# Second-network gate from SBUF sums, and five row blocks in place of six after the first two

## The chip, the cores and the metric

One Trainium2 chip, one core of it. The kernel is written in Python for Bass with the Tile layer, which allocates buffers and sets the semaphores. The metric is device time in microseconds (us), the median of a few runs. The engines are named as in the profile: PE is TensorE's matmul, PEld its weight load, DVE is VectorE, ACT is ScalarE, POOL is GpSimd, and SP is SyncE, which issues most DMAs.

## The reference, cut to what matters

Three networks follow one another on 2304 tokens (4 batches of 576) of 512 values.

```python
attn = softmax(mask(q @ k.T / 8))              # 8 heads of 64; 32 keys each, every key or every 4th
x = attn @ v                                   # as 2304 x 512
xn = x / sqrt(mean(x * x) + 1e-6) * rms_g      # first network
x = (silu(xn @ w_gate) * (xn @ w_val)) @ w_out     # 512 -> 1536 -> 512
logits = x @ w_gate2                           # the gate: 512 -> 8 experts
P = exp(logits - logits.max())                 # second network
for _ in range(8):
    P /= P.sum(1, keepdims=True) + 1e-9
    P /= P.sum(0, keepdims=True) + 1e-9
    P *= 2304 / 8
out = sum(P[:, e:e+1] * (relu(x @ w1[e]) @ w2[e]) for e in range(8))   # 512 -> 1024 -> 512
```

All is fp32. Matmul operands are split into a high and a low part in the rounded type fp32r, and a product is three matmuls: high by high, high by low, low by high.

## The kernel before, in words

**First phase.** Attention makes rows in tiles of 128 tokens (five tiles a batch, the fifth with 64), and writes them, normalised, transposed and split, into `xn`, the input of the first network. The first network works on blocks of tokens: two to a batch, 256 and 320 wide, eight in all. `gemm_h(blk, f)` makes one slice of 128 of the 1536 hidden values: 12 matmuls for `pg`, 12 for `pv` (L456), then Silu on ACT (L468), a product on DVE (L469), the high part on ACT (L470) and the low part on POOL (L471). `gemm_out(blk, c)` (L430) multiplies four such slices by `w_out`: 12 matmuls for each quarter `dc` of the 512 outputs, whose sums are collected in the tile `partial` by ACT (L439) or DVE (L441). After the third of three such chunks the sums are written to `x2d` in HBM (L443). Each matmul's moving operand is as wide as its block, and a block costs 12 x 24 + 3 x 4 x 12 = 432 matmuls.

**Order.** The first two blocks take turns chunk by chunk while their weights are still being converted (`split_double`: each half weight is loaded into a word buffer, and passes ACT, DVE and POOL by way of one of three buffers `m`; the conversion of the last ten weights loads from L345 into four word buffers). From block 2 on, a block's matmuls are the main line, and side lines are spread along them: the attention of the next block (`block_att`), a gate, and 24 steps of `weight_sums` a block. `weight_sums` has 64 items (load half a megabyte, three operations on POOL L645 to L653, one on DVE, store at L655) and takes 129 steps; it uses three large buffers, `kbd`, `vbd` and `conv`. Apart from SP's queue in the first part, which is in program order, a planner sets each engine's order when the kernel is built, by program order and its own estimates of when operands are ready; it brings ready work forward. On the chip each engine then runs its instructions in that order. `xn` of block i+2 has the buffer of block i.

**The gate.** `gate(blk)` takes 384 tokens. For each quarter it loads the sums back from `x2d` (L577, tile `sx`), makes the high part on ACT (L585) and the low part on POOL (L586), and multiplies both by the gate's weights (L592, tile `pl`, 16 outputs: a high and a low half). The 16 rows are copied (L599), transposed (L604) and written to `L2` (L605). Five gates run in the first phase; the sixth, `last_gate`, stands at the head of the second phase (loads L886, high parts on ACT L887, low parts on DVE L888, matmuls L898), since the last block's sums must first be in HBM.

**Second phase.** `gemm1` and `gemm2` (L1007, L1060) go through 48 units, 384 and 256 columns wide, with the gate's P computed on the side and needed from the fifth unit on. Weights are loaded and split unit by unit (L662, L676, L677), and stored split (L707). Its pools lie where those of the first phase lay, the tiles `h_a`, `h_s` over `kbd`, `vbd`, `conv` and `xn`, and wait for each of them.

Of the kernel before, what the change touches and what calls it, by code (L numbers as in the profile page):

```python
# [10 lines left out]
ALU = mybir.AluOpType  # L11
# [18 lines left out]
def attention_moe_kernel(  # L30
# [33 lines left out]
    wgs = cpool.tile([P, 4, NE], F32, name="wgs")  # L64
    wg = cpool.tile([P, 4, 2, NE], F32R, name="wg")
    L2 = cpool.tile([P, NTT, 16], F32, name="L2")
# [88 lines left out]
    def att_tile(n, xn, c0, bufs, after_qk=None, after_pv=None):  # L155
# [142 lines left out]
        for h in range(2):  # L298
            src = psT[:, halves[h]].rearrange("p (k n) -> p k n", k=2)
            hi, lo = (xn[:, 2 * h : 2 * h + 2, s, c0 : c0 + nn] for s in range(2))  # L300
# [21 lines left out]
    def split_double(pool, src, name, gk, number, hi_eng, lo_eng):  # L322
# [96 lines left out]

    def gemm_out(blk, c):  # L420
        tok0, n, _ = blocks[blk]
        if c == 0:
            partials[blk] = mpool.tile([P, 4, n], F32, tag=f"partial{blk % 2}", name=f"partial_{blk}", bufs=1)
        partial = partials[blk]
        for dc in range(4):
# [16 lines left out]
            if c == 2:  # L442
                nc.sync.dma_start(x2d[dc, :, tok0 : tok0 + n], partial[:, dc, :])  # L443
            yield

    def gemm_h(blk, f):
# [19 lines left out]
        h = mpool.tile([P, 2, 320], F32R, tag="h", name=f"h_{blk}_{f}", bufs=5)  # L466
        hf = mpool.tile([P, 320], F32, tag="hf", name=f"hf_{blk}_{f}", bufs=2)[:, :n]
# [104 lines left out]
    def gate(blk):  # L572

        pl = ps_o.tile([P, 512], F32, tag="o", name=f"pl_{blk}")
        def load(kt):
            st = stg.tile([P, 512], F32, tag="st", name=f"sx_{blk}_{kt}", bufs=3)[:, :TH]
            nc.sync.dma_start(st, x2d[kt, :, TH * blk : TH * blk + TH])  # L577
            return st

        st = load(0)  # L580
        yield
        k = 0
        for kt in range(4):
            hi, lo = (stg.tile([P, 512], F32R, tag="st", name=f"g{s}_{blk}_{kt}", bufs=3)[:, :TH] for s in range(2))
            nc.scalar.copy(hi, st)  # L585
            nc.gpsimd.tensor_tensor(out=lo, in0=st, in1=hi.bitcast(F32), op=ALU.subtract)  # L586
            for _ in range(3):
                yield
            if kt < 3:
                st = load(kt + 1)  # L590
            for x in (hi, lo):
                nc.tensor.matmul(  # L592
                    pl[:16, :TH], lhsT=wg[:, kt].rearrange("p s e -> p (s e)"), rhs=x, start=k == 0, stop=k == 7
                )
                k += 1
            for _ in range(3):
                yield
        lg = stg.tile([16, 512], F32, tag="st", name=f"lg_{blk}", bufs=3)
        nc.scalar.copy(lg[:, :TH], pl[:16, :TH])  # L599
        yield  # L600
        ptl = ps_o.tile([P, 512], F32, tag="o", name=f"ptl_{blk}")
        nt = TH // P
        for j in range(nt):
            nc.tensor.transpose(ptl[:, j * 16 : j * 16 + 16], lg[:, j * P : j * P + P], id16)  # L604
        nc.vector.tensor_copy(  # L605
            L2[:, nt * blk : nt * blk + nt, :], ptl[:, : nt * 16].rearrange("p (t e) -> p t e", e=16)
        )
# [126 lines left out]
    for b in range(B):  # L734
        blocks.append((b * S, 256, [(5 * b, 0), (5 * b + 1, 128)]))
# [499 lines left out]
```

## Time and profile before

| | us |
|---|---|
| median of 3 runs (2062.46 to 2068.68) | 2067.11 |
| the profiled execution's own time | 2064.67 |
| its span, first to last instruction | 2062.8 |
| PE busy in the span | 2005.0 (97%) |
| DVE, POOL, ACT busy | 1392.5, 1217.0, 1093.6 |

The times are those of whole executions; the span is what the profiler saw of one. The first phase ends, and the second begins, at 612 us of the span. A row of a view gives a group of instructions with their count, their busy time and the idle time ahead of them, or one stretch of time with each engine's busy part in it; PE's granted clock is given as a share of 2.4 GHz.

### The profile page before, as it was taken

How to read it: one execution, taken by the hardware profiler on the slowest of the kernel's cores; microseconds unless marked ns; L12 is line 12 of the kernel's file. 1: busy time of each engine (PE TensorE's matmuls, PEld its weight loads, DVE VectorE, ACT ScalarE, POOL GpSimd, SP SyncE). 2: the span in 40 equal slices, each digit the busy share in tenths (PEclk: the TensorE clock that was granted, in tenths of full speed). 3: DMA queues.
4: the chain of work that ended last, by engine and by line, in shares of the span. 5: the costliest groups of instructions: out<-in, count | busy, mean ns of one | idle time of the engine just before them, and what ended most of it. 6: DMA issues, size and time to landing. Idle time of an engine off the chain costs nothing.

```text
span 2062.8 us, 42661 instructions
## 1 busy us (share of the span) xinstructions
PE 2005.0 (97%) x16102; PEld 1967.9 (95%) x16102; DVE 1392.5 (68%) x2884; ACT 1093.6 (53%) x2408; POOL 1217.0 (59%) x1182
## 2 busy tenths in 40 slices
PE   6899999999999999999999999999999999999999
PEld 4788999999998999999999999999999999999999
DVE  7985443534347898787877676766776576667666
ACT  5664443433347566666665555555555654555453
POOL 4785555655646677778776454455545544554452
PEclk9999999999999999999999999999999999999999
DMA  9423777676556667877889667667677666566652
GB/s 270 168 83 125 252 238 245 227 239 248 212 181 250 234 242 290 305 278 275 296 321 359 198 197 233 205 203 226 220 247 268 220 205 203 181 198 205 204 175 82
DMA packets 210014, 464.68 MB, mean 225 GB/s; under 512 B 17168, under 2 KB 59920, under 8 KB 209808
## 3 DMA queue, kind: packets, MB, share of 16 engines
q1 hardware_dynamic: 202752, 442.97, 63.1%
q10 hardware_dynamic: 7056, 18.98, 2.8%
q8 instruction: 127, 2.08, 0.4%
q14 instruction: 79, 0.65, 0.1%
HBM read 349.16 MB, written 112.72 MB: 224 GB/s over the span
## 4 chain that ended last, share of the span: by engine, by line
PE 75%; DVE 8%; DMA 6%; ACT 4%; POOL 3%; issue 2%; SPq 1%; ACTq 0%; DVEq 0%; POOLq 0%
PE ya L1060 18%; PE pa L1007 17%; PE yb L1060 9%; PE pb L1007 8%; PE po L430 5%; PE pg L456 5%; PE pv L456 5%; PE pc L1007 4%; PE yc L1060 4%; DMA sx<-x2d 1%; DVE h_a L978 1%; DMA w0r<-in_w 1%; DMA x2d<-partial 1%; DMA kbd<-in_kt 1%; SPq L145 0%
## 5 line engine op out<-in xcount | busy, mean ns | idle before, releaser
L677 POOL TENSOR_TENSOR w_s<-w0s,w_s 128x512 fp32r<-128x512 f32 x192 | 261.0, 1360 | 91.3 <-ACT w_s L676 89.7
L986 POOL TENSOR_TENSOR h_s<-p,h_s 128x384 fp32r<-128x384 f32 x96 | 105.2, 1117 | 324.5 <-ACT h_s L985 271.1
L1096 DVE SCALAR_TENSOR_TENSOR acc<-ya,Pm,acc 128x256 f32<-128x256 f32 x510 | 221.8, 477 | 65.1 <-PE ya L1060 64.9
L677 POOL TENSOR_TENSOR w_a<-w0r,w_a 128x512 fp32r<-128x512 f32 x144 | 193.8, 1349 | 114.8 <-ACT w_a L676 108.1
L1007 PE MATMUL pa<-x_t,w_s 128*128 128x384 f32 x1152 | 224.3, 335 | 1.9 <-ACT p L1019 1.9
L1060 PE MATMUL ya<-w_t,h_s 128*128 128x256 f32 x1728 | 225.2, 282 | 0.6 <-ACT acc L1085 0.5
L1060 PEld LDWEIGHTS ya<-w_t,h_s 128*128 128x128 f32 x1728 | 218.8, 190 | 1.4 <-ACT acc L1085 0.8
L1007 PEld LDWEIGHTS pa<-x_t,w_s 128*128 128x128 f32 x1152 | 197.3, 188 | 2.3 <-ACT p L1019 2.1
L456 PE MATMUL pv<-xn,w_v 128*128 128x320 f32 (+1 forms) x1152 | 184.4, 302 | 10.7 <-DVE w_v L375 2.6
L456 PE MATMUL pg<-xn,w_g 128*128 128x320 f32 (+1 forms) x1152 | 183.7, 301 | 2.6 <-ACT hf L468 1.4
L430 PE MATMUL po<-h,w_o 128*128 128x320 f32 (+1 forms) x1152 | 175.0, 298 | 4.8 <-DVE partial L441 1.6
L456 PEld LDWEIGHTS pv<-xn,w_v 128*128 128x128 f32 x1152 | 164.2, 191 | 15.6 <-ACT hf L468 3.8
L676 ACT CAST w_s<-w0s 128x512 fp32r<-128x512 f32 x192 | 119.9, 625 | 108.2 <-PE pb L1007 66.4
L1096 DVE SCALAR_TENSOR_TENSOR acc<-yb,Pm,acc 128x256 f32<-128x256 f32 x258 | 109.7, 476 | 93.4 <-PE yb L1060 93.3
L456 PEld LDWEIGHTS pg<-xn,w_g 128*128 128x128 f32 x1152 | 163.3, 191 | 6.2 <-ACT hf L468 1.7
L430 PEld LDWEIGHTS po<-h,w_o 128*128 128x128 f32 x1152 | 159.4, 188 | 8.2 <-DVE partial L441 2.0
L471 POOL TENSOR_TENSOR h<-hf,h 128x256 fp32r<-128x256 f32 (+1 forms) x96 | 80.5, 840 | 100.2 <-ACT h L470 99.6
L986 POOL TENSOR_TENSOR h_s<-r,h_s 128x384 fp32r<-128x384 f32 x96 | 96.8, 1031 | 61.2 <-ACT h_s L985 57.3
L1060 PE MATMUL yc<-w_b,h_a 128*128 128x256 f32 x864 | 122.7, 283 | 0.0
L1060 PE MATMUL yb<-w_t,h_s 128*128 128x256 f32 x864 | 120.9, 281 | 0.0
L1060 PE MATMUL yb<-w_t,h_a 128*128 128x256 f32 x864 | 120.6, 282 | 0.3 <-DVE acc L1089 0.3
L1007 PE MATMUL pc<-x_b,w_a 128*128 128x384 f32 x576 | 116.4, 337 | 2.8 <-DVE h_s L986 2.7
(253 smaller groups left out, 4718.1 us busy)
## 6 DMA issues: line engine op xcount, KB each, us to landing
w_t<-split SPq DMA_DIRECT2D x128, 512.0 KB, 4.3
w0r<-in_w SPq DMA_DIRECT2D x96, 512.0 KB, 6.1
w0s<-sums SPq DMA_DIRECT2D x96, 512.0 KB, 7.5
w_b<-split SPq DMA_DIRECT2D x96, 512.0 KB, 3.8
split<-w_t SPq DMA_DIRECT2D x64, 512.0 KB, 2.9
split<-w_b SPq DMA_DIRECT2D x48, 512.0 KB, 3.6
w1r<-in_w SPq DMA_DIRECT2D x32, 512.0 KB, 5.4
w1s<-sums SPq DMA_DIRECT2D x32, 512.0 KB, 7.2
```

The costliest lines, as they stand in the source:

```text
L430: nc.tensor.matmul(po[:, :n], lhsT=ow[f][:, a, dc * P : dc * P + P], rhs=hs[blk, f][:, bb, :n], start=k == 0, stop=k == 11,)
L456: nc.tensor.matmul(ps[:, :n], lhsT=w[kt, fg][:, a, fo * P : fo * P + P], rhs=xn[:, kt, bb, :n], start=k == 0, stop=k == 11,)
L471: late_g = nc.gpsimd.tensor_tensor(out=h[:, 1, :n], in0=hf, in1=h[:, 0, :n].bitcast(F32), op=ALU.subtract)
L676: nc.scalar.copy(v[:, :, 0, :], src)
L677: lo_eng.tensor_tensor(out=v[:, :, 1, :], in0=src, in1=v[:, :, 0, :].bitcast(F32), op=ALU.subtract)
L978: nc.vector.scalar_tensor_tensor(out=h[:, 1, :], in0=src, scalar=0.0, in1=h[:, 0, :].bitcast(F32), op0=ALU.max, op1=ALU.subtract)
L986: eng.tensor_tensor(out=h[:, 1, :], in0=src, in1=h[:, 0, :].bitcast(F32), op=ALU.subtract)
L1007: nc.tensor.matmul(ps, lhsT=w1s[u, a][:, kt, hl, q * P : q * P + P], rhs=xc[b, kt][:, xl, :TH], start=fresh and k == 0, stop=k == 5, skip_ ...
L1060: nc.tensor.matmul(ps, lhsT=hh[u, a, q][:, hl, jj * P : jj * P + P], rhs=w2s[u, b][:, q, wl, :], start=fresh and k == 0 and jj != 1, stop= ...
L1096: nc.vector.scalar_tensor_tensor(out=dst, in0=ps, scalar=scale, in1=dst, op0=ALU.mult, op1=ALU.add)
```

## The change

The blocks from the second batch on are made of other tiles: 384, 320, 384, 320 and 320 tokens instead of six of 256 and 320, so seven blocks instead of eight (the first two stay). The gate works on a block, not on 384 tokens, from the block's sums while these are in SBUF: as each quarter is done, ACT and POOL split it into the block's own `xn`, whose rows are no longer needed (block 0's go through staging buffers instead). The sums of all blocks but the first share one buffer `partial`; the first block's lie in a part of `vbd`. `L2` holds the logits after the sum of their two halves, so the second phase needs no sum of its own. The sixth gate becomes the seventh block's own, in the first phase. `weight_sums` keeps its 24 steps a block. The word buffers of the last weights become three, in `kbd` and `conv`. Block 2's attention, now three tiles, runs beside the last chunks of blocks 0 and 1 rather than between them. In P's iterations four steps instead of three stand ahead of each matmul.

```diff
@@ split_double: word buffers of the last ten weights
-                if (2 * number + j) % 4 < 3:
-                    words = stg.tile([P, 512], U32, tag="st", name=f"sd_{name}_{j}", bufs=3)
-                else:
-                    words = conv[:, :512].bitcast(U32)
+                slot = (2 * number + j) % 3
+                words = (conv[:, :512] if slot == 2 else set0.spare[0][:, 512 * slot : 512 * slot + 512]).bitcast(U32)
@@ gemm_out
+    def split_partial(blk, dc, hi, lo):
+        src = partials[blk][:, dc, :]
+        nc.scalar.copy(hi, src)
+        nc.gpsimd.tensor_tensor(out=lo, in0=src, in1=hi.bitcast(F32), op=ALU.subtract)
+    def gate_step():
+        if gates and next(gates[0], run) is run:
+            gates.pop(0)
...
-            partials[blk] = mpool.tile([P, 4, n], F32, tag=f"partial{blk % 2}", name=f"partial_{blk}", bufs=1)
+            if blk == 0:
+                partials[blk] = set0.spare[1].rearrange("p (d n) -> p d n", d=4)
+            else:
+                partials[blk] = mpool.tile([P, 4, BIG[0]], F32, tag="partial", name=f"partial_{blk}", bufs=1)[:, :, :n]
...
             if c == 2:
                 nc.sync.dma_start(x2d[dc, :, tok0 : tok0 + n], partial[:, dc, :])
-            yield
+                if blk > 0:
+                    split_partial(blk, dc, xns[blk][:, dc, 0, :n], xns[blk][:, dc, 1, :n])
+            yield
+        if c == 2:
+            gates.append(gate(blk))
@@ gemm_h: hf moves to the staging buffers
-        hf = mpool.tile([P, 320], F32, tag="hf", name=f"hf_{blk}_{f}", bufs=2)[:, :n]
+        hf = stg.tile([P, 512], F32, tag="st", name=f"hf_{blk}_{f}", bufs=3)[:, :n]
@@ moe1_chunks
                 yield from gemm_h(blk, f)
+                if blk > 1:
+                    gate_step()
                 if pending:
                     yield from gemm_out(*pending.pop())
             pending.append((blk, c))
-        if chunks[-1] == (7, 2):
+        if chunks[-1] == (NB - 1, 2):
             yield from gemm_out(*pending.pop())
+            while gates:
+                gate_step()
@@ gate(blk): load, split and product of 384 tokens become a product from xn
-            st = stg.tile([P, 512], F32, tag="st", name=f"sx_{blk}_{kt}", bufs=3)[:, :TH]
-            nc.sync.dma_start(st, x2d[kt, :, TH * blk : TH * blk + TH])
-            nc.scalar.copy(hi, st)
-            nc.gpsimd.tensor_tensor(out=lo, in0=st, in1=hi.bitcast(F32), op=ALU.subtract)
+                rhs = parts[kt][:, n * hl : n * hl + n] if blk == 0 else xns[blk][:, kt, hl, :n]
+                nc.tensor.matmul(
+                    pl[:16, :n], lhsT=wg[:, kt].rearrange("p s e -> p (s e)"), rhs=rhs,
+                    start=kt == hl == 0, stop=kt == 3 and hl == 1,
+                )
...
+            nc.vector.reduce_sum(
+                out=L2[a:b, t0 + j : t0 + k, :], in_=pair.rearrange("p t s e -> p t e s"), axis=AX.X
+            )
@@ blocks
-        blocks.append((b * S, 256, [(5 * b, 0), (5 * b + 1, 128)]))
-        blocks.append((b * S + 256, 320, [(5 * b + 2, 0), (5 * b + 3, 128), (5 * b + 4, 256)]))
+    for tiles in ((0, 1), (2, 3, 4), (5, 6, 7), (8, 9, 10), (11, 12, 13), (14, 15, 16), (17, 18, 19)):
...
+    BIG = (384, 320)
@@ order
-    run(moe1_chunks([(0, 2)]))
     next_psum()
-    run(block_att(2))
-    run(moe1_chunks([(1, 2)]))
+    third = block_att(2)
+    for step_, _ in enumerate(moe1_chunks([(0, 2), (1, 2)])):
+        if step_ % 2 == 0 and step_ < 10 or step_ > 10:
+            next(third, None)
+    run(third)
...
-    for i in range(2, 8):
+    for _ in range(3):
+        gate_step()
+    for i in range(2, NB):
         sides = [(some(sgen1, 24), 24)]
...
@@ side(): the last gate goes
-    def last_gate():
...
-        yield from last_gate()
-        nc.vector.tensor_tensor(out=Pm, in0=L2[:, :, 0:8], in1=L2[:, :, 8:16], op=ALU.add)
+        for _ in range(4):
+            yield
```

## Rows read from the trace of the kernel before

**Rows 1.** Page, part 5, costliest groups: one of three such groups (pg, pv, po)

```profile
L456 PE MATMUL pg<-xn,w_g 128*128 128x320 f32 (+1 forms) x1152 | 183.7, 301 | 2.6 <-ACT hf L468 1.4
```

**Rows 2.** Chain that ended last, in time: start us, us, what (widths 256, 320, 384)

```profile
372.86 1.44 PE pv L456 x12
...
589.76 1.76 PE pg L456 x12
...
699.39 2.08 PE pa L1007 x12
```

**Rows 3.** Stretches at the phases' boundary: engines' busy us, PE's clock, DMA share, GB/s

```profile
612.00:622.80 10.80, 10.80 (x63) 10.52 (x61) 2.08 (x4) 4.60 (x10) 3.61 (x4) 1.00 1.04 402
622.80:629.60 6.80, 2.03 (x6) 0.35 (x5) 5.13 (x5) 5.56 (x12) 6.80 (x6) 0.75 0.82 300
629.60:633.10 3.50, 3.47 (x11) 3.47 (x12) 3.42 (x7) 3.49 (x9) 3.50 (x3) 0.50 0.87 287
```

**Rows 4.** Chain that ended last, 600 to 645 us

```profile
610.66 8.43 DMA x2d<-partial
...
619.15 5.65 DMA sx<-x2d
...
626.41 3.17 DVE xg L888 x2
```

**Rows 5.** Timeline of PE, 622 to 640 us: start, us, what, idle before and releaser

```profile
625.39 0.35 PE L898 MATMUL pl_last<-xg,wg 128*16 128x384 f32 x1 [2.55 <-ACT xg L887]
...
629.93 3.71 PE L1007 MATMUL pa<-x_b,w_s 128*128 128x384 f32 x12
```

**Rows 6.** Groups by line and form: the gate's matmuls, in the phase and at its end

```profile
L592 PE MATMUL pl<-g,wg 128*16 128x384 f32 x40 | 10.7, 337 | 0.0
...
L898 PE MATMUL pl_last<-xg,wg 128*16 128x384 f32 x8 | 3.2, 447 | 4.8 <-ACT xg L887 2.6 <-DVE xg L888 2.2
```

**Rows 7.** Waits, 180 to 640 us: total us, times, longest

```profile
ACT g L585 <- DMA sx<-x2d: 22.0, 8, 5.9
```

**Rows 8.** Waits of PE alone, 180 to 612 us

```profile
PE psR L286 <- ACT psX L278: 2.6, 1, 2.6
PE psXT L297 <- DVE xs L291: 1.9, 2, 1.1
```

**Rows 9.** Tile sx: low parts on POOL and on DVE, ns min/median/max

```profile
L586 POOL TENSOR_TENSOR g<-sx,g x20: 1007/1018/1470, 204.2 to 579.3; 128x384 fp32r<-128x384 f32 x20
...
L888 DVE TENSOR_TENSOR xg<-sx,xg x4: 549/1364/1627, 625.4 to 630.6; 128x384 fp32r<-128x384 f32 x4
```

**Rows 10.** Timeline of SP, 137 to 172 us: loads into one word buffer of four

```profile
143.72 0.33 SPq L345 DMA_DIRECT2D conv<-in_w_val  x1
...
151.68 0.33 SPq L345 DMA_DIRECT2D conv<-in_w_val  x1
```

**Rows 11.** Timeline of ACT, 140 to 153 us: first use of one buffer m, twice

```profile
142.91 0.44 ACT L355 ACTIVATE conv<-sd_v 128x256 f32<-128x256 f32 x1 [0.45 <-DVE w_g L375]
...
151.07 0.44 ACT L355 ACTIVATE conv<-sd_v 128x256 f32<-128x256 f32 x1 [0.94 <-DVE w_v L375]
```

**Rows 12.** Timeline of PE, 165 to 210 us: tile 6's transposes, block 2's first matmul

```profile
190.11 0.60 PE L297 MATMUL psXT<-cst,xs 128*128 128x128 f32 x4
...
192.17 0.38 PE L456 MATMUL pg<-xn,w_g 128*128 128x256 f32 x1
```

**Rows 13.** Timeline of DVE, 186 to 222 us: last writes of tiles 6 and 7

```profile
192.40 0.62 DVE L307 TENSOR_TENSOR xn<-psXT,xn 128x256 fp32r<-128x256 f32 x1
...
219.96 0.63 DVE L307 TENSOR_TENSOR xn<-psXT,xn 128x256 fp32r<-128x256 f32 x1 [1.17 <-ACT xn L306]
```

**Rows 14.** A stretch ahead of block 2, columns as in Rows 3

```profile
180.00:190.00 10.00, 9.44 (x71) 9.24 (x71) 2.80 (x8) 2.21 (x8) 3.83 (x6) 1.00 0.49 155
```

**Rows 15.** Lines L653 and L655, weight sums: the last item's operation; stores' landing

```profile
L653 POOL TENSOR_TENSOR kbd<-kbd x11: 732/738/1190, 224.5 to 565.0; 128x256 f32<-128x256 f32 x11
...
DMA to landing us min/median/max: 2.6/3.9/7.6
```

More of the change, by code (lines that the diff above doesn't have):

```diff
@@ L299, in att_tile @@
             src = psT[:, halves[h]].rearrange("p (k n) -> p k n", k=2)
-            hi, lo = (xn[:, 2 * h : 2 * h + 2, s, c0 : c0 + nn] for s in range(2))
+            dst = xn() if callable(xn) else xn
+            hi, lo = (dst[:, 2 * h : 2 * h + 2, s, c0 : c0 + nn] for s in range(2))
             if h == 0:
@@ L598, in gate @@
[L598 to L607, printed above, removed]
+        tok0, n, _ = blocks[blk]
@@ new lines, in gate, with product @@
+        if blk == 0:
+            parts = [stg.tile([P, 512], F32R, tag="st", name=f"gp_{blk}_{kt}", bufs=3) for kt in range(3)]
+            parts.append(parts[0])
+        pool, kw = (ps_o, dict(tag="o")) if blk < NB - 1 else (ps_a, dict(tag="single", bufs=1))
+        pl = pool.tile([P, 512], F32, name=f"pl_{blk}", **kw)
+        def product(kt):
+            for hl in range(2):
+                rhs = parts[kt][:, n * hl : n * hl + n] if blk == 0 else xns[blk][:, kt, hl, :n]
[3 more added lines that the diff above has]
+                )
@@ new lines, in gate @@
+        if blk == 0:
+            for kt in range(3):
+                split_partial(blk, kt, parts[kt][:, :n], parts[kt][:, n : 2 * n])
+            yield
+            product(0)
+            parts[3] = stg.tile([P, 512], F32R, tag="st", name=f"gp_{blk}_3", bufs=3)
+            split_partial(blk, 3, parts[3][:, :n], parts[3][:, n : 2 * n])
+            yield
+        for kt in range(1 if blk == 0 else 0, 4):
+            product(kt)
+        yield
+        off = tok0 % P
+        lg = stg.tile([16, 512], F32, tag="st", name=f"lg_{blk}", bufs=3)
@@ new lines, in gate @@
+        if off:
+            nc.gpsimd.memset(lg[:, :off], 0.0)
+        nc.scalar.copy(lg[:, off : off + n], pl[:16, :n])
+        yield
+        ptl = pool.tile([P, 512], F32, name=f"ptl_{blk}", **kw)
+        t0, nt = tok0 // P, -(-(off + n) // P)
+        spans = []
+        for j in range(nt):
+            w = min(P, off + n - P * j)
+            nc.tensor.transpose(ptl[:w, j * 16 : j * 16 + 16], lg[:, j * P : j * P + w], id16)
+            spans.append((off if j == 0 else 0, w))
+        j = 0
@@ L733, in attention_moe_kernel @@
     blocks = []
-    for b in range(B):
-        blocks.append((b * S, 256, [(5 * b, 0), (5 * b + 1, 128)]))
-        blocks.append((b * S + 256, 320, [(5 * b + 2, 0), (5 * b + 3, 128), (5 * b + 4, 256)]))
+    for tiles in ((0, 1), (2, 3, 4), (5, 6, 7), (8, 9, 10), (11, 12, 13), (14, 15, 16), (17, 18, 19)):
+        n, tl = 0, []
+        for tn in tiles:
+            tl.append((tn, n))
+            n += P if tn % 5 < 4 else P // 2
+        blocks.append((sum(bl[1] for bl in blocks), n, tl))
+    NB = len(blocks)
+    BIG = (384, 320)
     xns = {}
@@ L740, in block_att, with xn @@
         tok0, n, tl = blocks[i]
-        xns[i] = mpool.tile([P, 4, 2, n], F32R, tag=f"xn{i % 2}", name=f"xn_{i}", bufs=1)
+        def xn():
+            if i not in xns:
+                xns[i] = mpool.tile([P, 4, 2, BIG[i % 2]], F32R, tag=f"xn{i % 2}", name=f"xn_{i}", bufs=1)
+            return xns[i]
         for tn, c0 in tl:
@@ L947, in side @@
             nc.vector.reduce_sum(out=csum, in_=Pm.rearrange("p t e -> p e t"), axis=AX.X)
-            for _ in range(3):
+            for _ in range(4):
                 yield
```

82 lines of the change are left out of this document (18 added, 64 removed).

## The prediction

> **What bounds the kernel now.** I read the page first: PE is busy 97% of the span, and part 2 shows it at 9 tenths or more in every slice after the first two. So time is won in two ways alone, by less PE work or by closing the few gaps in PE's stream. The work that the change touches is three groups of 1152 matmuls, 3456 in all [rows 1], that is 8 blocks of 432. The chain gives what a closed group of twelve costs: 1.44 us at 256 columns, 1.76 at 320, 2.08 at 384 [rows 2], so 120.0, 146.7 and 173.3 ns a matmul. Each 64 columns add 26.7 ns, and what is left at no columns is 120.0 - 4 x 26.7 = 13.3 ns: a fixed cost of every matmul.
>
> The windows show the largest gap. From 622.8 to 629.6 us, just after the second phase begins, PE is busy 2.03 of 6.80 us at a granted clock of 0.75, and from 629.6 to 633.1 the clock is 0.50, its level of 1.2 GHz, after PE had been idle [rows 3]. The chain names the cause: the last sums' way to HBM (8.43 us), back (5.65), and their split [rows 4]. PE stood 4.8 us ahead of the last gate's matmuls [rows 6], and the twelve matmuls behind them took 3.71 us [rows 5] against 2.08 [rows 2]: 4.8 + 1.6 = 6.4 us lost.
>
> Elsewhere in the first phase the waits view shows ACT held 22.0 us by the gate's loads [rows 7], but PE itself waited little from 180 to 612 us: 2.6 us for a square on ACT and 1.9 for the normalised rows are its longest [rows 8]. So that ACT wait is mostly off the path.
>
> **The change, part by part.**
>
> *Fewer matmuls.* Seven blocks for eight make 432 fewer, over the same columns: 432 x 13.3 = 5.76 us less PE work. In the stretch of blocks 2 and later PE has no cover for it to vanish in, so I take it whole: **-5.8**. The Trainium skill, TensorE: Matmul & The Clock Gate, section "Back-to-back issue gap", gives the gap between warm matmuls as N / 2.4 + 2.5 ns. By it the saving would be an estimated 432 x 2.5 = 1.1 us, and the whole sum below -3.6 instead of -8.3. The fixed part measured here, over three widths, is 13.3 ns; so the trace doesn't agree with the 2.5.
>
> *The last gate from SBUF.* Four stores to HBM stay, but nobody waits for them at the boundary; four loads of 0.2 MB go, and ACT no longer stands in its queue ahead of the evictions of `pa`. In their place the last block's quarters are split as they come, a copy of about 0.5 us on ACT and a subtraction of about 1.0 us on POOL [rows 9], while PE has the second phase's first unit, 84 matmuls of 173 ns, 14.6 us, to go on with. The matmuls themselves weigh the same: 48 of 384 columns cost 8.3 us, 56 of the new widths 8 x (120 + 4 x 146.7 + 2 x 173.3) ns = 8.4; three more transposes and the added waits in P's loop I put at 0.3. **+0.4**. The 6.4 us of the gap could all come back.
>
> *The weight sums run over.* They take 129 steps; six blocks of 24 gave 144, five give 120. Before, the last item ended at 566 us [rows 15], 46 us ahead of the boundary. Now five of 64 items are left, and their POOL and DVE work is tied behind the last `gemm_h`. That is 15 operations of 0.74 us on POOL [rows 15], 11.1 us, three loads and five stores of 0.52 MB, 4.2 MB against the 0.8 MB of the gate's loads that go. They land where the DMA engines are already at 1.04 and move 402 GB/s [rows 3]: 3.4 MB more is 8.5 us of their time. Behind them in the queues stand the second unit's weight loads on SP and splits on POOL, which PE needs some 15 us after the boundary. Also `h_a`, `h_s` lie over `kbd`, `vbd` and `conv` and wait for the last stores, of up to 7.6 us each [rows 15]; other slots, over `xn` and the attention's buffers, are free at once, so the first of them need not wait. Lower bound nothing (all within the 14.6 us), upper the full 8.5 us and the half clock again, 1.6. I take 2.5, as the first unit covers most of it. Boundary together: -6.4 + 2.5 = **-3.9**. The Trainium skill, GPSIMD Engine Reference, section "Key points", says that GpSimd shares its SBUF interfaces with VectorE and contends with its two-input instructions. The trace agrees: a two-input subtraction on DVE ranged from 549 to 1627 ns [rows 9] where POOL was busy throughout [rows 3]. Four such operations stretched to the longest would add an estimated 4.3 us, with a sum of -4.0; that is weight for the rival that the boundary refills.
>
> *ACT and POOL in the blocks.* 28 copies and subtractions of block width replace 24 of each sort at 384; their inputs come from a DVE addition instead of a DMA of several us. PE's waits of 1.9 us [rows 8] may go in part: between 0 and -1.9, **-1.0**. The single `partial` buffer must be read out before the next block's first sums; four slices of `gemm_h`, 96 matmuls of 147 ns or 14 us, lie between, against stores that land in 8.43 us at the slowest [rows 4]: nothing. If a store were later than that, PE's evictions would wait for it on ACT.
>
> *Three word buffers for four.* Now one of the four comes round in 8.0 us [rows 10], 2.0 us a half weight. If the same round held three, each half would take 2.65, and the nine halves up to the last `w_val` would come 6 us later: the upper bound. But the buffers `m` are three already, and one of them is reused after 8.2 us, with ACT waiting for DVE to leave it [rows 11]: that ring is the tighter one, 2.7 us a half. So near the lower end of 0: **+0.5**.
>
> *Three attention tiles before block 2.* Block 2 needed two, and started 2.1 us after the last of them was transposed [rows 12], with PE never idle. Tile 7 now stands ahead too; in the trace it ended 27.6 us behind tile 6 [rows 13]. Cover after 192.2 us: block 1's last sums, 48 x 146.7 = 7.0 us, tile 7's own matmuls, an estimated 3.0 us (five groups like the 0.60 us of its transposes), and block 0's gate, 8 x 0.12 = 1.0: until 203.2 us. At the pace of before tile 7 would end at 220.6, idle 17.4 us; at best it is hidden. In the ten us ahead of block 2 DVE, ACT and POOL were busy 2.80, 2.21 and 3.83 of 10 [rows 14]: the tile's pace there was set by its place in the order, not by an engine. In the new order its instructions precede the end of block 1, and PE has nothing better. I estimate 12.3 us for it, less than half, so **+1.5**.
>
> **Sum:** -5.8 + 0.4 - 3.9 - 1.0 + 0.5 + 1.5 = -8.3 us, on the profiled execution 2064.7 - 8.3 = 2056.4. That execution is 2.4 us below the median of the three runs, so as a median 2058.8.
>
> **The rivals.**
>
> *A. The boundary refills (same).* The five late items and the loads behind them cost PE about what the last gate did. For: DMA share 1.04 there; against: 14.6 us of independent matmuls. Time: 2058.8 + 3.9 = 2062.7.
>
> *B. All gaps close (faster).* The 6.4 us come back whole, the psXT wait of 1.9 goes, tile 7 and the words are hidden, and so is the single PE wait of 2.6 us [rows 8] with a half clock behind it of 1.6: that one came from `weight_sums`, whose first items now run elsewhere. -5.8 + 0.4 - 6.4 - 1.9 - 4.2 = -17.9: 2049.2. Against: planned orders make new gaps where they close old ones.
>
> *C. The attention is the bound before block 2 (slower).* Tile 7 keeps its 27.6 us: PE idles 17.4 us and pays 1.6 at the half clock, 17.5 more than the 1.5 taken: 2076.3. It decides from about 8 us of idle, tile 7's end at 212, where the gain is gone; from 218 the change is slower by over 0.3%.
>
> *D. The fixed part stays (same).* If what is constant in a matmul were not paid by the count, wider blocks would bring nothing: 2058.8 + 5.8 = 2064.6. Against: three widths lie on one line [rows 2]. This is where the section on the issue gap, cited above, would lead.
>
> **How the numbers follow.** 0.3% is 6.2 us, about what a measurement of this kernel can tell from no change. Forecast 0.42, own range 2053 to 2061; A 0.22; B 0.16; C 0.15; D 0.05. Faster: the forecast and B, 0.58. Same: A and D, 0.27. Slower: C, 0.15. The range holds the forecast, A, D, most of B and none of C's far end: 2048 to 2070.
>
> **What would show it.** In the changed profile: 3024 matmuls in the three groups, twelve still at 1.44, 1.76 and 2.08 us; no idle PE ahead of `pl` at the boundary, and a clock of 1.00 there; weight sums (L653's successor) after the last `gemm_h`, and PE waits, if any, for splits on POOL or `w0r`, `w1s` landings (A); the stretch from block 1's last slice to block 2's first matmul without idle PE (C would show PE waiting for `xn` or `xs`); loads into word buffers still 2 to 2.7 us apart. The prediction would be wrong if PE stood for more than 5 us ahead of block 2, or if the second phase's first units waited longer than the last gate had made them.

## The result and the profile after

The change made the kernel slower: a median of 2085.77 us over 4 runs (2081.62 to 2089.48) against 2067.89 us for the kernel before (4 runs). The ratio is 1.0101, with a 95% interval of 1.0083 to 1.0119. The forecast was 2058.8 us, with a range of 2048 to 2070.

The page of the changed kernel, head and part 1, then two groups of part 5, which answer to [rows 1], and the group `po` of the kernel before:

```profile
span 2087.7 us, 41709 instructions
...
PE 2011.7 (96%) x15681; PEld 1973.5 (95%) x15681; DVE 1388.8 (67%) x2866; ACT 1088.1 (52%) x2383; POOL 1214.6 (58%) x1181
...
L442 PE MATMUL po<-h,w_o 128*128 128x320 f32 (+2 forms) x1008 | 177.3, 324 | 11.8 <-POOL h L487 5.2
L472 PE MATMUL pg<-xn,w_g 128*128 128x320 f32 (+2 forms) x1008 | 180.3, 321 | 4.9 <-DVE hf L485 2.1
```

```profile
L430 PE MATMUL po<-h,w_o 128*128 128x320 f32 (+1 forms) x1152 | 175.0, 298 | 4.8 <-DVE partial L441 1.6
```

Three groups of 1008 are the 3024 matmuls forecast. The number behind the last bar is PE's idle time ahead of the group: `po` waited 4.8 us before and waits 11.8 us now, 5.2 of them for POOL. The chain that ended last shows what twelve matmuls cost (start us, us, what), beside a group of the second phase:

```profile
223.44 2.12 PE pv L472 x12
...
305.94 1.76 PE pv L472 x12
...
695.38 2.08 PE pa L1014 x12
```

Against [rows 2], 320 columns cost the same; 384 columns cost 2.12 us in the first phase and 2.08 in the second.

The boundary of the phases is where the time went. The timeline of PE from 595 to 660 us (start, us, what, idle before and releaser in brackets):

```profile
604.67 1.97 PE L442 MATMUL po<-h,w_o 128*128 128x320 f32 x6 [2.78 <-POOL h L487]
...
611.37 3.57 PE L442 MATMUL po<-h,w_o 128*128 128x320 f32 x12 [2.45 <-DVE partial L453]
...
634.63 0.59 PE L932 MATMUL pr<-idp,gm 128*1 128x128 f32 x2 [3.99 <-DMA idp<-in_consts]
...
657.78 2.50 PE L1067 MATMUL ya<-w_b,h_a 128*128 128x256 f32 x10 [14.66 <-ACT h_a L984]
```

The timeline of ACT, 655 to 660 us, says what `h_a` waited for:

```profile
657.24 0.87 ACT L984 ACTIVATE h_a<-pc 128x384 fp32r<-128x384 f32 x2 [16.17 <-DMA sums<-conv]
```

The chain from 612 to 662 us shows how that came about:

```profile
612.99 7.68 DMA sums<-vbd
620.69 8.04 DMA vbd<-in_w
...
628.79 0.75 POOL vbd L681
...
646.36 0.68 POOL conv L689
647.04 0.32 POOL kbd L689
647.36 9.78 DMA sums<-conv
657.24 0.50 ACT h_a L984
657.78 4.21 PE ya L1067 x18
```

A store has to leave `vbd` before the next item is loaded there. The late items' operations stand between splits of weights on POOL, and the last store from `conv`, that of the last item but one, lands at 657.1 us. Only then may ACT write the first `h_a`, which lies over that buffer. The tile view of `sums`, 590 to 665 us, answers to [rows 15]: a store's landing had a median of 3.9 us over the first phase of the kernel before and has 7.2 here.

```profile
L691 SPq DMA_DIRECT2D sums<-conv x2: 319/365/411, 618.1 to 647.4; - x2
...
DMA to landing us min/median/max: 3.3/7.2/10.5
```

Windows of the changed kernel (us, then busy us of PE, PEld, DVE, ACT, POOL with counts, PE's granted clock, DMA share, GB/s):

```profile
220.00:575.00 355.00, 355.00 (x3595) 343.02 (x3595) 143.99 (x292) 130.37 (x265) 193.79 (x249) 1.00 0.60 206
575.00:600.00 25.00, 22.42 (x149) 21.48 (x147) 22.27 (x32) 11.85 (x27) 19.33 (x18) 1.00 0.79 269
600.00:620.00 20.00, 13.46 (x56) 12.02 (x57) 7.19 (x8) 6.03 (x12) 18.48 (x22) 0.66 0.84 274
620.00:640.00 20.00, 14.85 (x74) 13.59 (x73) 7.85 (x18) 10.14 (x20) 10.96 (x13) 0.87 0.90 345
640.00:660.00 20.00, 5.34 (x24) 5.02 (x24) 4.55 (x9) 3.23 (x9) 7.72 (x8) 0.67 0.68 236
```

The gap of before at 623 to 633 us [rows 3] is closed: `pl` of the last block has no idle PE ahead of it. Three others took its place, each with a stretch at the lower level of the clock behind it. The middle of the first phase got better: PE is never idle from 220 to 575 us, against 348.06 busy of 355 before, and both waits of [rows 8] are gone.

To add this up I use one measure: **lost time** is the length of a stretch less what the matmuls that start in it cost at the full clock, 13.3 ns and 26.7 ns for each 64 columns [rows 2] (short ones at a flat 60 ns, the attention's, several of which run side by side, at 12 ns; these are the same in all kernels). By this measure all matmuls cost 1952.2 us before and 1946.8 after, 5.4 us less. Lost, in us, in the profiled executions:

| kernel | 0–220 | 220–575 | 575–700 | 700–2000 |
|---|---|---|---|---|
| before | 58.8 | 26.8 | 12.2 | 8.1 |
| after | 65.0 | 17.7 | 41.4 | 12.3 |
| after − before | +6.2 | −9.1 | **+29.2** | +4.2 |

The differences make +30.5 us, less 5.4 of matmuls +25.1; the spans differ by 24.9 (2087.7 − 2062.8). The medians differ by 17.9: the profile after is 3.7 us above its median, that of before 3.2 below its own. How finely a column can be read: eight kernels with one and the same program up to about 200 us, of those below, lost 61.3 to 65.5 us in the first. A row is no count of idle time: after the change PE is never idle from 220 to 575 us, and the 17.7 us stand for what these prices leave out, so that only differences between kernels say something.

### The profile page after: what moved, and what is told of

It is laid out like the page before. It is cut to its first block, busy times and chain, and to the rows that moved or that the text cites. A ratio compares the mean times of both kernels' runs of the same rounds, so it can differ in the third digit from the quotient of the medians.

```text
span 2087.7 us, 41709 instructions
## 1 busy us (share of the span) xinstructions
PE 2011.7 (96%) x15681; PEld 1973.5 (95%) x15681; DVE 1388.8 (67%) x2866; ACT 1088.1 (52%) x2383; POOL 1214.6 (58%) x1181
## 4 chain that ended last, share of the span: by engine, by line
PE 79%; DVE 6%; DMA 6%; POOL 3%; issue 2%; ACT 2%; SPq 1%; ACTq 0%; DVEq 0%; POOLq 0%
PE ya L1067 17%; PE pa L1014 16%; PE yb L1067 9%; PE pb L1014 8%; PE pg L472 6%; PE pv L472 6%; PE po L442 6%; PE pc L1014 4%; PE yc L1067 4%; DMA w0r<-in_w 2%; POOL w_s L713 1%; POOL w_t L713 1%; DMA xr<-x2d 1%; PE psS L175 1%; PE psX L239 1%
## 5 line engine op out<-in xcount | busy, mean ns | idle before, releaser
L442 PE MATMUL po<-h,w_o 128*128 128x320 f32 (+2 forms) x1008 | 177.3, 324 | 11.8 <-POOL h L487 5.2
L472 PE MATMUL pg<-xn,w_g 128*128 128x320 f32 (+2 forms) x1008 | 180.3, 321 | 4.9 <-DVE hf L485 2.1
L472 PE MATMUL pv<-xn,w_v 128*128 128x320 f32 (+2 forms) x1008 | 180.2, 321 | 4.3 <-DVE w_v L373 2.5
L472 PEld LDWEIGHTS pv<-xn,w_v 128*128 128x128 f32 x1008 | 158.8, 191 | 8.9 <-DVE w_v L373 3.6
L472 PEld LDWEIGHTS pg<-xn,w_g 128*128 128x128 f32 x1008 | 158.5, 192 | 8.6 <-DVE hf L485 2.8
L487 POOL TENSOR_TENSOR h<-hf,h 128x320 fp32r<-128x320 f32 (+2 forms) x84 | 77.6, 925 | 131.6 <-ACT h L486 131.5
L993 POOL TENSOR_TENSOR h_s<-r,h_s 128x384 fp32r<-128x384 f32 x96 | 96.3, 1025 | 63.6 <-ACT h_s L992 59.3
L1067 PE MATMUL ya<-w_b,h_a 128*128 128x256 f32 x864 | 115.7, 285 | 14.7 <-ACT h_a L984 14.7
L1067 PEld LDWEIGHTS ya<-w_b,h_a 128*128 128x128 f32 x864 | 112.5, 193 | 15.0 <-ACT h_a L984 15.0
```

The lines of the kernel that those rows point to most:

```text
L442: nc.tensor.matmul(po[:, :n], lhsT=ow[f][:, a, dc * P : dc * P + P], rhs=hs[blk, f][:, bb, :n], start=k == 0, stop=k == 11,)
L472: nc.tensor.matmul(ps[:, :n], lhsT=w[kt, fg][:, a, fo * P : fo * P + P], rhs=xn[:, kt, bb, :n], start=k == 0, stop=k == 11,)
L487: late_g = nc.gpsimd.tensor_tensor(out=h[:, 1, :n], in0=hf, in1=h[:, 0, :n].bitcast(F32), op=ALU.subtract)
L993: eng.tensor_tensor(out=h[:, 1, :], in0=src, in1=h[:, 0, :].bitcast(F32), op=ALU.subtract)
L1067: nc.tensor.matmul(ps, lhsT=hh[u, a, q][:, hl, jj * P : jj * P + P], rhs=w2s[u, b][:, q, wl, :], start=fresh and k == 0 and jj != 1, stop= ...
```

## The experiments

Lost time by stretch, in us, beside the ratio to the kernel before with its interval:

| kernel | 0–220 | 220–575 | 575–700 | 700–2000 | ratio |
|---|---|---|---|---|---|
| after, 30 steps a block | 64.4 | 31.2 | 10.3 | 16.2 | 1.0036 (1.0023–1.0049) |
| before, 20 steps a block | 57.5 | 21.3 | 35.8 | 10.0 | 1.0073 (1.0058–1.0088) |
| after, late items in own tiles | 62.4 | 17.5 | 21.7 | 10.8 | 0.9981 (0.9971–0.9990) |
| the same again, another chip | 65.5 | 17.7 | 21.2 | 11.2 | 0.9995 (0.9983–1.0008) |
| own tiles, late items in units 1–5 | 63.0 | 17.6 | 20.8 | 18.6 | 1.0026 (1.0014–1.0038) |
| own tiles, 16 steps in the last block | 61.3 | 17.5 | 27.0 | 13.7 | 1.0017 (1.0003–1.0031) |
| after, last 16 items left out | 63.6 | 17.6 | 17.1 | 16.5 | 0.9986 (0.9969–1.0002) |
| after, attention as before | 67.2 | 18.1 | 34.0 | 13.6 | 1.0081 (1.0066–1.0096) |
| own tiles, block 0's gate later | 63.2 | 18.7 | 19.6 | 14.2 | 0.9996 (0.9982–1.0010) |
| own tiles, third attention early | 63.7 | 17.6 | 20.7 | 11.9 | 0.9995 (0.9986–1.0005) |
| own tiles, `hf` own, four `h` | 61.9 | 21.0 | 23.7 | 12.7 | 1.0016 (1.0007–1.0025) |
| before, `hf` shared | 81.1 | 43.0 | 14.5 | 12.6 | 1.0184 (1.0162–1.0206) |
| before, three word buffers | 63.2 | 27.5 | 10.6 | 8.2 | 1.0001 (0.9992–1.0011) |
| own tiles, P's loop as before | 63.4 | 17.6 | 23.0 | 11.8 | 1.0015 (1.0006–1.0024) |

**The overrun undone.**

```diff
-        sides = [(some(sgen1, 24), 24)]
+        sides = [(some(sgen1, 30), 30)]
```

> The changed kernel, with 30 instead of 24 weight-sum steps to a block, so that all 129 end inside the first phase (5 x 30 = 150). Theory 1 (the five items left over make the loss at the boundary): PE's stall of 14.7 us ahead of the first ya falls under 3 us, the half clock from 634 to 662 us goes for the most part, and the time falls by 20 to 30 us, to 2056 to 2066. Theory 2 (the last block's gate and its splits on POOL and ACT, now at the end of the first phase, make it): the waits of 2.45 to 2.78 us ahead of po and the late first ya stay, and the time stays within 8 us of the changed kernel's 2086. Theory 3 (larger buffers and another layout of SBUF make it, whatever work is late): the first h still waits for a buffer, the time stays within 8 us too.

Measured 2077.53 us. At the boundary theory 1 holds: the stall ahead of the first `ya` is gone and the loss there falls from 41.4 to 10.3 us. But the time fell only by 0.65% of the kernel before, some 13 us, since 220 to 575 us lost 13.5 us more. Its window, against the 355.00 busy above:

```profile
220.00:575.00 355.00, 345.92 (x3485) 332.32 (x3472) 143.71 (x299) 126.51 (x258) 211.62 (x272) 0.99 0.67 230
...
600.00:620.00 20.00, 18.36 (x120) 17.32 (x119) 8.15 (x13) 10.71 (x22) 17.80 (x17) 1.00 0.75 249
...
640.00:660.00 20.00, 15.49 (x103) 14.65 (x102) 17.16 (x33) 13.62 (x33) 13.48 (x12) 1.00 0.71 275
```

So a good part of the better middle of the changed kernel was bought with the overrun. Per column of a block's width, 24 steps over a mean of 345.6 columns are 0.069, and 30 are 0.087; before, 24 over 288 were 0.083. The losses rise in that order: 17.7, 31.2 and, between them, 26.8 us.

**The overrun alone, in the kernel before.**

```diff
-        sides = [(some(sgen1, 24), 24)]
+        sides = [(some(sgen1, 20), 20)]
```

> The kernel before, with 20 instead of 24 weight-sum steps to a block: 6 x 20 = 120 of 129, so that the same five items are left over, and nothing else is changed. Theory 1 (the overrun alone makes the loss): 15 to 30 us slower than the kernel before, about 2083 to 2098, with the first h of the second phase waiting for a store of a sum. Theories 2 and 3 (the last gate's new place, or the new layout of SBUF): within 6 us of the kernel before, 2062 to 2074.

Measured 2086.01 us, 16 above the kernel before, with none of the change in it. Its density is again 0.069 (20 over 288), and 220 to 575 us lost 21.3 instead of 26.8: thinner sums alone bring 5.5 of the changed kernel's 9.1 us. Timelines of PE and of ACT, 600 to 655 us:

```profile
647.31 2.38 PE L898 MATMUL pl_last<-xg,wg 128*16 128x384 f32 x6 [21.35 <-ACT xg L887]
```

```profile
646.75 1.34 ACT L887 CAST xg<-sx 128x384 fp32r<-128x384 f32 x3 [16.63 <-DMA sums<-conv]
```

The store from `conv`, again that of the last item but one, holds the first tile of the same pool (here `xg`, the split for the last gate). Theories 2 and 3 fall as causes of the large loss.

**The buffer taken out of it.**

```diff
-            t = bufs[i % 3].rearrange("p (i n) -> p i n", i=2)
+            if i < 59:
+                t = bufs[i % 3].rearrange("p (i n) -> p i n", i=2)
+            else:
+                t = wx.tile([P, 2, 512], F32R, tag="w", name=f"ws_{i}").bitcast(F32)
```

> The changed kernel, with the five weight-sum items that are left over in tiles of the weight pool instead of in kbd, vbd and conv; their loads, sums and stores stay, at the same place in the order. If the dear part of the overrun is the wait of the first h for a buffer that a store still reads (16 us on ACT, 14.7 us on PE), that wait goes and the time falls by 10 to 20 us, to 2066 to 2076. If it is the load on POOL and on the DMA queues, the wait moves to the weights of the first units, and the time stays within 6 us of 2086. If the larger ring of weight tiles delays loads, it is slower.

Measured 2065.86 us: with the same late work at the same place, the loss at the boundary is halved, and 1.2% of the time, some 25 us by the ratios, is back. ACT's timeline and the windows, as above:

```profile
625.16 0.49 ACT L987 ACTIVATE h_a<-pc 128x384 fp32r<-128x384 f32 x1
```

```profile
600.00:620.00 20.00, 14.47 (x65) 13.10 (x65) 8.92 (x10) 3.10 (x7) 19.28 (x25) 0.66 0.83 285
620.00:640.00 20.00, 18.15 (x105) 16.53 (x104) 10.53 (x20) 14.79 (x33) 14.94 (x14) 1.00 1.03 404
640.00:660.00 20.00, 20.00 (x143) 19.91 (x142) 17.09 (x41) 17.97 (x42) 14.00 (x12) 1.00 0.60 231
```

The first `h_a` is written at 625.2 instead of 657.2 us. The DMA share of 1.03 at 620 to 640 us shows that the transfers are as dense as the prediction feared, and PE goes through them with 18.15 of 20 us busy. What stays is 600 to 620 us. This is the one version that came out ahead of the kernel before, so it ran again:

> The changed kernel with the left-over items in own tiles once more, on another chip and with more rounds, since it is the one version that came out faster than the kernel before. If that holds, the ratio is 0.997 to 0.999 again; if it was the luck of one chip, the interval takes in 1.

Measured 2067.76 us, a ratio of 0.9995 whose interval takes in 1. It beats the changed kernel by 1.1 to 1.2%; against the kernel before it is the same within 0.3%.

**What holds `po` at 595 to 612 us.** Two kernels on top of the own tiles: the late items moved into the second phase (`u_now` is the unit's number), and fewer steps beside the last block (nine items are then late, all in own tiles).

```diff
-            nxt = load(i + 1) if i + 1 < len(items) else None
-            yield
+            if i >= 59:
+                while u_now[0] < i - 58:
+                    yield
+                t = load(i)
+                nxt = None
+                for _ in range(6):
+                    yield
+            else:
+                nxt = load(i + 1) if i < 58 else None
+                yield
...
-    run(sgen1)
...
             next(prep, None)
+            next(sgen1, None)
```

> The changed kernel with the five left-over items in tiles of the weight pool and moved out of the boundary: one each in units 1 to 5 of the second phase, load and operations a third of a unit apart; their sums are read in units 12 to 15. With those items at the boundary but in own tiles PE still lost 22 us from 575 to 700 us, half of it ahead of the sums po, which waited for POOL and DVE. If that is the items' POOL and DVE work running ahead of the splits of h, the loss falls to about 10 us, as with 30 steps to a block, while the stretch from 220 to 575 us keeps its low loss of 17 us: 8 to 14 us less than with own tiles alone, 2053 to 2059, faster than both kernels by 0.4 to 0.8%. If it is the last gate's splits (the rival), the loss stays near 20 us and the time within 4 us of 2066. If POOL is short in the second phase, units 1 to 5 give back what the boundary gains.

Measured 2073.19 us. The theory falls: the first late item is now loaded at 637 us and worked on from 652 us, and yet the loss from 575 to 700 us is 20.8 us, as with all of them at the boundary (21.7 and 21.2). Units 1 to 5 and their successors gave 7 us away.

```diff
-        sides = [(some(sgen1, 24), 24)]
+        sides = [(some(sgen1, 24 if i < NB - 1 else 16), 24 if i < NB - 1 else 16)]
```

> The changed kernel with the items that run late in own tiles, and 16 instead of 24 weight-sum steps in the last block: nine items are late instead of five. With 24 steps PE lost 13 us from 585 to 620 us, ahead of po, against 3 us where the last block had 9 steps (30 to a block) and against 1.4 in the kernel before (9 as well). If the sums beside the last block make that loss, it falls to 7 to 9 us, and the late items, which cost nothing more after 620 us so far, leave a gain of 3 to 6 us: ratio 0.995 to 0.9965. If each item costs about 1 us of PE wherever it stands, the loss only moves behind 620 us and the time stays: ratio 0.997 to 0.999.

Measured 2073.5 us. The loss from 585 to 620 us falls from 13.4 to 11.5 us, but that from there to 700 us rises from 6.8 to 13.8, with 8.4 instead of 3.0 from 660 to 680 us alone. The second theory was the nearer: what the last block won, the boundary behind it lost, and more.

**The sums out of the last block and the boundary.** The items run over 12 chunks instead of 16:

```diff
-        items = [(w, ch, k) for ch in range(NCH) for w in range(2) for k in range(2)]
+        items = [(w, ch, k) for ch in range(12) for w in range(2) for k in range(2)]
```

> The changed kernel with the last 16 of 64 weight-sum items left out (the last four chunks read the sums of the four before them, so the output is another): four blocks of 24 steps hold the other 48, none stands beside the last block and none is late. What is left is the rest of the change at its best. If the sums alone make the boundary dear, PE's lost time from 575 to 700 us falls from 41 to about 10 us, as with 30 steps a block, with 220 to 575 us still at 17 us: 2051 to 2058, a ratio of 0.992 to 0.995. If the last gate and its splits of the sums in SBUF cost something of their own there, the loss stays at 15 us or more, and PE waits ahead of pl or po for POOL. Against own tiles alone (0.998) the difference is the price of the 16 items: by about 1.1 us each of the runs so far that are beside the last block, 9 to 13 us.

Measured 2066.17 us, above the 2051 to 2058 expected. Against own tiles beside it (2067.76 us) the 16 items are worth about 2 us, which the two intervals can't tell from nothing, and not 9 to 13. The boundary's windows:

```profile
600.00:620.00 20.00, 19.20 (x106) 17.52 (x104) 5.77 (x13) 9.38 (x21) 8.94 (x10) 0.91 0.68 244
620.00:640.00 20.00, 17.73 (x94) 17.41 (x94) 15.03 (x29) 14.16 (x33) 11.76 (x11) 0.83 0.82 288
```

The waits of `po` shrink, so the sums beside the last block made most of them. Its group from 575 to 625 us, with own tiles, here, and in the kernel before:

```profile
L442 PE MATMUL po<-h,w_o 128*128 128x320 f32 x95 | 19.9, 363 | 9.6 <-POOL h L487 4.8 <-DVE partial L453 3.9 <-ACT h L486 0.8
...
L442 PE MATMUL po<-h,w_o 128*128 128x320 f32 x95 | 17.1, 334 | 2.1 <-POOL h L487 1.8 <-DVE partial L453 0.3
...
L430 PE MATMUL po<-h,w_o 128*128 128x320 f32 x116 | 18.7, 310 | 0.5 <-DVE partial L441 0.3 <-POOL h L471 0.2
```

But the boundary still loses 17.1 us, 11.0 of them from 620 us on, in the first units' own waits, and from 700 us on 16.5 us are lost instead of 11.2. Its PE timeline:

```profile
632.28 2.29 PE L1014 MATMUL pa<-x_t,w_s 128*128 128x384 f32 x6 [2.27 <-ACT pq L1026]
...
657.03 1.33 PE L1014 MATMUL pb<-x_t,w_a 128*128 128x384 f32 x6 [2.14 <-DVE u L1035]
```

The last gate's gap is gone and little is won by it: 10.3 us (30 steps) and 17.1 us here stand against 12.2 before. Why the second phase loses more without the items is open.

**The start of block 2.** Three kernels: the third block's attention back in its old place; the first gate moved behind the start of block 2 (it then splits rows that the weight sums have overwritten, so block 0's gate is another); the attention stepped from the first step on.

```diff
-    third = block_att(2)
-    for step_, _ in enumerate(moe1_chunks([(0, 2), (1, 2)])):
-        if step_ % 2 == 0 and step_ < 10 or step_ > 10:
-            next(third, None)
-    run(third)
+    run(moe1_chunks([(0, 2)]))
+    next_psum()
+    run(block_att(2))
+    run(moe1_chunks([(1, 2)]))
```

> The changed kernel with the third block's attention where it stood before: after block 0's last slice and ahead of block 1's, instead of interleaved with both. PE's lost time up to 220 us was 58.8 us before and 65.0 after. If the interleaving makes the loss around 190 to 210 us (5 us more there than before), the time falls by 3 to 6 us, to 2080 to 2083. If the third tile makes it, wherever it stands, the time is the same within 2 us, or longer by up to 15 us, since tile 7 then stands ahead of block 1's last slice in full.

```diff
-    for _ in range(3):
-        gate_step()
```

> The changed kernel with the left-over items in own tiles, and block 0's gate no longer ahead of block 2 but in its slices, with the gates behind it. PE idled 2.69 us there ahead of the gate's product, which waited for ACT, with 3.4 us at half clock behind it. If that wait is the dearer start of block 2 (4.7 us more lost from 190 to 220 us than before), the time falls by 2 to 4.5 us, to 2061 to 2064. If the third attention tile makes it, PE waits for the tile instead, and the time stays within 1.5 us of 2066.

```diff
-        if step_ % 2 == 0 and step_ < 10 or step_ > 10:
-            next(third, None)
+        next(third, None)
```

> The changed kernel with the left-over items in own tiles, and a step of the third block's attention beside every step of the two last slices, from the first on, instead of five steps beside the first ten and then every one. The changed kernel loses about 8 us of PE from 185 to 222 us, the one before 3 to 4; with the attention all in one piece it was 10. If tile 7 ends too late for block 2, an earlier start ends it earlier: 3 to 5 us lost there, ratio 0.001 to 0.002 under own tiles alone. If what is lost is the work that tile 7 puts on ACT and DVE there, it only moves to 160 to 190 us, and the ratio stays within 0.001.

From 180 to 220 us the kernel before lost 3.8 us, the changed one 9.1, with own tiles 8.5; the attention in its old place 10.1, the gate moved 8.7, the early start 6.7 (and 5.2 instead of 3.5 from 160 to 190). None brings the 3.8 back, and no time moved by as much as 0.3%: the place of the gate or of the steps doesn't make the cost. That the third tile makes it is argued and not shown, since no run took the tile away.

**Buffers.** `hf` is in shared buffers after the change, which the prediction didn't price.

```diff
-        hf = mpool.tile([P, 320], F32, tag="hf", name=f"hf_{blk}_{f}", bufs=2)[:, :n]
+        hf = stg.tile([P, 512], F32, tag="st", name=f"hf_{blk}_{f}", bufs=3)[:, :n]
```

> The kernel before, with hf (the product of silu and value) in the three shared buffers st, as the change has it, instead of two of its own; nothing else is changed. PE's lost time from 40 to 80 us was 17.7 us before and 20.8 after. If the shared buffers make that difference, this one is 2 to 5 us slower than before; the stretch from 220 us may lose more, as the gate's loads and splits take the same buffers. If the other order of the first instructions makes it, the time is the same within 2 us, or slower in the later stretch alone.

Measured 2107.64 us, far more than either theory: in the kernel before, the words and the gate's loads use the same three buffers. PE's longest wait, from its timeline:

```profile
183.82 2.93 PE L456 MATMUL pv<-xn,w_v 128*128 128x256 f32 x12 [10.46 <-ACT hf L468]
```

Since the change takes both out of these buffers, sharing costs it little: 40 to 80 us lost 17.7 us before, 22.5 here and 19 to 21 with the change. The reverse edit on own tiles:

```diff
-        h = mpool.tile([P, 2, BIG[0]], F32R, tag="h", name=f"h_{blk}_{f}", bufs=5)
-        hf = stg.tile([P, 512], F32, tag="st", name=f"hf_{blk}_{f}", bufs=3)[:, :n]
+        h = mpool.tile([P, 2, BIG[0]], F32R, tag="h", name=f"h_{blk}_{f}", bufs=4)
+        hf = mpool.tile([P, BIG[0]], F32, tag="hf", name=f"hf_{blk}_{f}", bufs=2)[:, :n]
```

> The changed kernel with the left-over items in own tiles, and hf back in two buffers of its own as before; for the room, four h buffers instead of five. In the kernel before, moving hf to the shared buffers raised PE's lost time from 40 to 80 us from 17.7 to 22.5 us; the kernels with the change lose 19 to 21 there. If the sharing makes that, the stretch falls to about 17.5 us and the time by 2 to 3 us against own tiles alone (ratio 0.998 to the kernel before), to a ratio of 0.9965 to 0.997. If four h buffers hold PE up, with po or pg waiting for h, it is slower than own tiles alone.

The stretch fell to 17.4 us as expected, but four `h` buffers cost more (80 to 100 us lost 7.1 instead of 1.6): 2072.4 us in all.

The word buffers of the change, in the kernel before:

```diff
-                if (2 * number + j) % 4 < 3:
-                    words = stg.tile([P, 512], U32, tag="st", name=f"sd_{name}_{j}", bufs=3)
-                else:
-                    words = conv[:, :512].bitcast(U32)
+                slot = (2 * number + j) % 3
+                words = (conv[:, :512] if slot == 2 else set0.spare[0][:, 512 * slot : 512 * slot + 512]).bitcast(U32)
```

> The kernel before, with the words of the last ten weights in conv and two halves of kbd as the change has them, three buffers instead of four. The prediction took +0.5 us, at most +6. If the scratch m is the tighter ring, the time is within 1.5 us of before; if the words are, 3 to 6 us slower, with PE waiting for w_v from 145 to 165 us; if kbd, still read by the attention, holds the first loads, slower still.

Measured 2068.08 us, a ratio of 1.0001: no difference that can be told. (Its profiled execution lost 7.5 us from 140 to 160 us, where that of the kernel before lost 3.8; the interval, up to 1.0011 or 2.3 us, leaves room for part of that.)

**P's loop**, three steps a turn instead of four, on own tiles:

```diff
-            for _ in range(4):
+            for _ in range(3):
                 yield
             pc = ps_o.tile([P, 512], F32, tag="o", name=f"pc_{it}")
```

> The changed kernel with the left-over items in own tiles, and three steps instead of four in each turn of P's loop, as before. All kernels with the change lose 4.5 to 8 us of PE from 760 to 800 us, where acc is scaled by P on DVE and h_s stands behind it; the kernels without it lose 2 to 4. If P, one step a turn later, makes that, the stretch loses 2 to 4 us and the ratio goes 0.001 to 0.002 under that of own tiles alone (0.9981 and 0.9995). If the different start of the second phase makes it, the stretch stays at 4.5 to 8 us and the ratio where it was.

From 760 to 800 us 3.4 us were lost, as in the kernel before (3.7), so the local reading holds; 660 to 680 us (4.3 instead of 2.8 to 3.0) and 900 to 1000 us (2.8 instead of 0) lost it again, and the time, 2069.35 us, is no better.

## Why the prediction was wrong

*The step that failed is the weight sums' overrun, +2.5 us in the boundary's −3.9.* The boundary measured +29.2. That five items are left over, that they are tied behind the last `gemm_h`, and that `h_a` and `h_s` lie over `kbd`, `vbd` and `conv` was all in the text. What was wrong is the sentence that other slots are free at once, "so the first of them need not wait". The first `h_a` was the one over `conv`, behind the store of the last item but one: 16.17 us on ACT, 14.66 on PE, longer than the last gate had made PE wait, which is one of the prediction's own signs of being wrong. The bounds, 8.5 us of transfers and 1.6 of clock, priced the DMA engines' time and not the chain of store, load, POOL and store through three buffers. Giving the items other buffers took 20 us off the boundary; moving them out of it as well brought it no lower (20.8 against 21.2 to 21.7).

*The density of the sums was not counted.* The same 24 steps beside a wider block put more items beside the last block (24 steps where the kernel before had 9 left), and these held `po`, which waited 9.6 us in own tiles, 2.1 without them and 0.5 before. The same thinning took 5.5 us off the middle in the kernel before, so it is most of the 9.1 us won there, which the text gave to other reasons (−1.0 for ACT and POOL). The other 3.6 us are more than that term, and no run shows which part of the change makes them; with denser sums the middle of the change is no better than that of before (31.2 at 0.087 against 26.8 at 0.083). One price for an item doesn't hold: with 30 steps 64 instead of 55 stores of sums start from 220 to 575 us, for 13.5 us, while the 16 items left out at the end were worth about 2 us in all, which the intervals can't tell from nothing.

*The last gate's gap, −6.4.* It closed, but new waits took most of it: with no late sums, in the run with 30 steps, the boundary lost 10.3 us against 12.2. Rival A named such a refill, at the price of the last gate, so at a boundary no dearer than before; the measured one was 29.2 us dearer.

*Fewer matmuls, −5.8.* The count and the 13.3 ns held at 320 columns. The 864 matmuls of 384 columns in the first phase took 2.12 us for twelve instead of 2.08, 3.3 ns each or 2.9 us, so about half of the term was left; why these are slower than the second phase's is open. Rival D is not borne out: the fixed part of 13.3 ns stands. The 2.5 ns of the Trainium skill, TensorE: Matmul & The Clock Gate, section "Back-to-back issue gap", which that section gives for an isolated matmul and not for a stream of weight loads and matmuls, fit these rows no better than those of before; so they were no price for this saving.

*Three attention tiles, +1.5.* From 180 to 220 us 9.1 us were lost instead of 3.8, so about 5 us more, with the sign right. The gate's first product and block 2's first matmul, the last writes of tiles 6 and 7, timelines of PE and DVE, which answer to [rows 12, 13]:

```profile
196.86 0.40 PE L604 MATMUL pl<-gp,wg 128*16 128x256 f32 x2 [2.69 <-ACT xn L306]
...
208.56 0.44 PE L472 MATMUL pg<-xn,w_g 128*128 128x384 f32 x1 [0.46 <-ACT xn L306]
```

```profile
196.82 0.64 DVE L307 TENSOR_TENSOR xn<-psXT,xn 128x256 fp32r<-128x256 f32 x1
...
210.82 0.63 DVE L307 TENSOR_TENSOR xn<-psXT,xn 128x256 fp32r<-128x256 f32 x1 [0.19 <-ACT xn L306]
```

Tile 7 ends 14.0 us behind tile 6 (27.6 before, 12.3 estimated), so rival C's 17 us didn't come. In this execution the cost is the single wait of 2.69 us, 3.4 us at half clock behind it, and small waits; with the gate moved, waits of 1.38 us for `rs` and 1.36 us for `xs`, both of the attention, stood in its place.

*The rest.* Three word buffers: nothing that the medians show, as said (+0.5). The last gate's quarters take 0.46 us on ACT and 0.87 on POOL at 320 columns, no more than priced; its whole term (+0.4) no run isolates. Left out of the sum were `hf` in shared buffers, 1 to 3 us from 40 to 80 us, the wait of 3.99 us of `pr` for `idp` (before, `pr` came ten us later, at 644.24 us, and waited for nothing), and some 3 to 4 us given back from 760 to 800 us and after.

So what is left with own tiles: 5.4 us of matmuls by count and 9.1 to 9.3 in the middle won; 3.6 to 6.7 at the start, 9.0 to 9.5 at the boundary and 2.7 to 3.1 in the second phase lost. With the last 16 items left out it is 4.8, 4.9 and 8.4 us lost. Either way that is the kernel before within 0.3%, which the runs show at ratios of 0.998 to 1.000.

## What to carry to other kernels

A side job that is paced in steps per block changes when the blocks change: count the steps again, per unit of time and against the end of the phase, and price the last item as a chain through its buffers up to whoever takes the buffer next, since the first taker may get the worst slot. Where a stretch becomes free of waits, look at what work has left it; here more than half of the middle's gain was work that had moved to the end. And a gap that closes on a full machine is worth its length only if the next wait in line is shorter.

## What was not expected of the hardware

- The DMA queues at a share of 1.03 (404 GB/s, 620 to 640 us, own tiles) left PE 18.15 of 20 us busy; the same items cost 14.66 us in one wait when a buffer hung on one of their last stores, which took 9.78 us to land at a share of 0.68 (640 to 660 us). In the kernel before with 20 steps that store landed in 3.9 us, and PE still waited 21.35 us: the chain ahead of that store, and not its landing, was the cost there.
- Twelve matmuls of 384 columns took 2.12 us in the first phase and 2.08 in the second; at 320 columns both kernels show 1.76.
- PE's clock fell to its level of 1.2 GHz behind waits of less than 3 us, too: after the change, in windows of 2 us, the grant was 1.00 up to 602 us, 0.50 from 604 to 616 us and 1.00 again from 618 us, and the longest wait from 600 to 620 us was 2.78 us, with PE busy 13.46 of 20.
